# The order of four VectorE products in a frequency-domain convolution, with an MLP behind it

## The chip, the cores and the metric

The kernel runs on one core of a Trainium2 chip. A core has TensorE (matrix products, written to PSUM), VectorE, ScalarE, GpSimd, and SyncE, whose queue issues all DMAs here. Each engine works through its instructions in program order and waits on semaphores for the others. The metric is the device time of one execution in microseconds (us), the median of several runs. A profile of one execution of each kernel is available.

## The reference

Four sequences of 12480 tokens with 128 channels are gated, convolved with a filter made by a small network, gated again, and put through an MLP. The convolution is done by FFT over the sequence:

```python
h_filt = (np.maximum(pos_emb @ w1, 0.0) @ w2) * window      # (S, D), S = 12480, D = 128
u = x * v                                                   # (B, S, D), B = 4
Uf = np.fft.rfft(u, n=2 * S, axis=1)
Hf = np.fft.rfft(h_filt, n=2 * S, axis=0)
y = np.fft.irfft(Uf * Hf[None, :, :], n=2 * S, axis=1)[:, :S, :]
a = x * y                                                   # out of the convolution
h = a @ w_in                                                # 128 -> 2048
out = (h * np.clip(h + 3.0, 0.0, 6.0) / 6.0) @ w_out        # 2048 -> 128
```

## The kernel before

The FFT of length 12544 = 64 x 196 is done as two stages of matrix products with twiddle tables, there and back. Of the 196 frequencies of the long factor, 99 are kept (`K2`), four to a chunk (`CH`), so there are 25 chunks; the last has three. The channels and the batch make 8 groups of 128 columns (2 halves of the sequence x 2 batches x 32 channels). Each group is one *period* (`period`, line 601) of 25 chunks, so that the code around the change runs 200 times.

One chunk (`chunk`, line 629) does this:

- `spectra` (L488) calls `second_stage`: TensorE multiplies four frequencies of the group with the table `tab` (L301) into one PSUM bank, the tile `t`. Its pool is called `s2` and has two buffers, so that chunk n writes the bank of chunk n-2. A bank row holds four frequencies of 128 columns; partitions 0 to 63 hold one part of each complex number and 64 to 127 the other.
- `products` (L503) multiplies with the filter's spectrum `h`. ScalarE first copies the two partition halves crosswise into another PSUM bank, `sw` (L499, and L500 with the sign turned; its pool has one buffer). VectorE then forms four products: `q` and `a` from the spectrum itself (`uv`), `q2` and `a2` from the swapped spectrum (`sv`). `q` and `q2` have 256 columns, `a` and `a2` 512. They read one operand from PSUM and `h` from SBUF. GpSimd adds `q` into half of `a`, `q2` into half of `a2`, and `a2` into `a` (L527). In the first period VectorE does the last of these adds in two chunks of three (L533), a chunk later.
- `third_stage` (L541), three or four chunks later, is the way back: TensorE multiplies `a` with the same table (L546), and ScalarE writes the result over the group's place in `z` (L550).

The order is written out by hand; the instructions are scheduled as they stand. In one chunk: `products` of chunk n, a `third_stage`, `spectra` of chunk n+1, a further `third_stage`. Between the chunks `period` spreads the work of the neighbouring groups: `back` (L552) transposes the finished group before (TensorE L557, ScalarE's copy L560); `visit` (L457) does the first stage of the next group (TensorE L282, ScalarE's copy L294); `fourth_stage` and `results` (L575, L594, L596) finish the group before; `gate_next` (L446) forms x * v on GpSimd (L453) and issues the next loads; `weight` (L647) splits the MLP's weights on VectorE (lines 225 to 247) and ScalarE (L243). `load_h` (L475) issues the two DMAs for the filter's spectrum three chunks ahead, behind the four products; `load_tab` (L465) loads the tables.

Ahead of the periods, `filter` computes the filter's spectrum (to about 158 us); behind them come `last_turn` and the MLP (`Moe.run`, L843), which takes the rest of the time.

The buffers that matter here: `s2` two banks, `sw` one, `s3` two, `ts` three (L267); `a` four tiles in SBUF, `a2`, `q` and `q2` three each; `h` four.

Of the kernel before, what the change touches and what calls it, by code (L numbers as in the profile page):

```python
# [38 lines left out]
GB = 2  # L39
# [211 lines left out]
class Conv:  # L251
# [251 lines left out]
    def products(self, item):  # L503

        nc, P = self.nc, 128
        g, c, kw, t, tab = item
        sw = self.swapped(t, kw)
        hs = self.hs.pop(0)
        a = self.pr.tile([P, CH, 2 * GB, G], F32, tag="a", name="pa", bufs=4)
        a2 = self.pr.tile([P, CH, 2 * GB, G], F32, tag="a2", name="pa2")  # L510
        q = self.pr.tile([P, CH, GB, G], F32, tag="q", name="pq")
        q2 = self.pr.tile([P, CH, GB, G], F32, tag="q2", name="pq2")
        uv = t.rearrange("p (k s g) -> p k s g", k=CH, g=G)[:, :kw]
        sv = sw.rearrange("p (k s g) -> p k s g", k=CH, g=G)[:, :kw]

        def h(ci, si, m):
            return hs[:, ci, :kw, si, :].unsqueeze(2).to_broadcast([P, kw, m, G])

        mul, add = ALU.mult, ALU.add
        nc.vector.tensor_tensor(out=q[:, :kw], in0=uv[:, :, :GB], in1=h(0, 1, GB), op=mul)  # L520
        nc.vector.tensor_tensor(out=a[:, :kw], in0=uv, in1=h(0, 0, 2 * GB), op=mul)  # L521
        nc.vector.tensor_tensor(out=q2[:, :kw], in0=sv[:, :, :GB], in1=h(1, 1, GB), op=mul)
        nc.vector.tensor_tensor(out=a2[:, :kw], in0=sv, in1=h(1, 0, 2 * GB), op=mul)
        self.load_h()

        def plus(x, y):
            nc.gpsimd.tensor_tensor(out=x, in0=x, in1=y, op=add)  # L527

        plus(a[:, :kw, GB:], q[:, :kw])
        plus(a2[:, :kw, GB:], q2[:, :kw])  # L530
        if self.sum:
            s, s2 = self.sum
            nc.vector.tensor_tensor(out=s, in0=s, in1=s2, op=add)  # L533
        self.sum = None
        if g == 0 and c % 3:
            self.sum = a[:, :kw], a2[:, :kw]
        else:
            plus(a[:, :kw], a2[:, :kw])
        return g, c, kw, tab, a
# [355 lines left out]
```

## Time and profile before

| | |
|---|---|
| median of 3 runs | 3170.02 us (3169.38 to 3170.16) |
| profiled execution | 3166.51 us, of which span 3164.7 us |
| TensorE busy | 3114.2 us (98%) |
| ScalarE busy | 2351.7 us (74%) |
| VectorE busy | 2305.8 us (73%) |
| GpSimd busy | 2079.2 us (66%) |
| mean granted TensorE clock | 0.998 |

The span runs from the first instruction of the program to the end of the last. Lines of the profile name an instruction by its line in the kernel's file (L301). A row of a group gives its engine (PE is TensorE, PEld its weight load, DVE is VectorE, ACT is ScalarE, POOL is GpSimd, SP is SyncE), the operation, the tiles written and read, the shape and the count; then the busy time in us, the mean of one in ns, and behind the second bar the time for which the engine stood idle just before, with what ended it. In the order of time a row starts with its start and its length in us, and square brackets hold the idle time ahead of it. What ended a wait is worked out from semaphores: of several, the one that came last is named, and that may be wrong. In names, `pa` is the tile `a` or `a2`, `pq` is `q` or `q2`, `s` a bank of `s2` or `s3`, and `sw` the swapped one.

### The profile page before, as it was taken

What the parts mean: (1) busy time and instruction counts of PE and PEld (TensorE: products, weight loads), DVE (VectorE), ACT (ScalarE), POOL (GpSimd) and SP (SyncE); (2) the same over time, 40 slices, a digit from 0 to 9 for tenths busy, and PEclk for the clock granted to TensorE, in tenths of its full rate; (3) what the DMA queues carried; (4) which work ended last, traced back from release to release, by engine and by line L of the source; (5) the groups of instructions that cost most, each with busy time, mean ns of one, the idle gap of its engine ahead of it and who ended that gap; (6) DMA issues with size and microseconds to landing.
All of it is one profiled execution on the core that took longest, in us unless ns stands there. A gap on an engine that the chain in (4) does not pass through costs nothing.

```text
span 3164.7 us, 53332 instructions
## 1 busy us (share of the span) xinstructions
PE 3114.2 (98%) x19916; PEld 2633.9 (83%) x19916; DVE 2305.8 (73%) x2707; ACT 2351.7 (74%) x3039; POOL 2079.2 (66%) x1240
## 2 busy tenths in 40 slices
PE   9989999999999999999999999999999999999999
PEld 8978888888887788888888888888888888888887
DVE  4467666767654777777777777777777777777776
ACT  2367767767766777878787777777777877777777
POOL 1188777777874666666666666666666666666666
PEclk9999999999999999999999999999999999999999
DMA  6688888787855111111111110111111111111110
GB/s 236 211 205 230 228 230 234 218 238 221 228 172 202 54 36 35 38 42 35 35 40 31 41 41 30 41 39 32 41 36 35 39 32 41 38 33 40 40 31 24
DMA packets 232273, 304.66 MB, mean 96 GB/s; under 512 B 38055, under 2 KB 159310, under 8 KB 231118
## 3 DMA queue, kind: packets, MB, share of 16 engines
q1 hardware_dynamic: 232014, 301.26, 32.6%
q8 instruction: 157, 2.57, 0.3%
q14 instruction: 102, 0.84, 0.1%
HBM read 224.87 MB, written 76.28 MB: 95 GB/s over the span
## 4 chain that ended last, share of the span: by engine, by line
PE 68%; POOL 0%; DVE 0%; ACT 0%; DMA 0%; issue 0%; ACTq 0%
PE acc L827 11%; PE acc L823 11%; PE acc L824 11%; PE ph L788 11%; PE ph L790 11%; PE ph L789 11%; PE ts L575 0%; PE s L557 0%; PE ts L557 0%; POOL pa L527 0%; DMA yd<-y 0%; POOL glo L812 0%; DVE y L596 0%; ACT o L594 0%; ACT ghi L810 0%
## 5 line engine op out<-in xcount | busy, mean ns | idle before, releaser
L812 POOL TENSOR_TENSOR glo<-g,ghi 128x1024 fp32r<-128x1024 f32 x588 | 1404.4, 2397 | 761.2 <-ACT ghi L810 761.0
L800 DVE SCALAR_TENSOR_TENSOR g<-r,ph 128x1024 f32<-128x1024 f32 (+1 forms) x784 | 949.7, 1211 | 408.7 <-ACT r L798 408.3
L798 ACT ACTIVATE r<-ph,three 128x1024 f32<-128x1024 f32 (+1 forms) x784 | 871.1, 1111 | 273.6 <-PE ph L790 273.4
L810 ACT CAST ghi<-g 128x1024 fp32r<-128x1024 f32 (+1 forms) x784 | 811.1, 1035 | 1.9 <-DVE g L800 1.0
L788 PE MATMUL ph<-xhi,win_hi 128*128 128x512 f32 (+1 forms) x1568 | 608.5, 388 | 0.0
L789 PE MATMUL ph<-xlo,win_hi 128*128 128x512 f32 (+1 forms) x1568 | 608.4, 388 | 0.0
L790 PE MATMUL ph<-xhi,win_lo 128*128 128x512 f32 (+1 forms) x1568 | 608.3, 388 | 0.0
L824 PE MATMUL acc<-ghi,wout_lo 128*128 128x512 f32 (+1 forms) x1568 | 608.0, 388 | 0.0
L823 PE MATMUL acc<-ghi,wout_hi 128*128 128x512 f32 (+1 forms) x1568 | 607.9, 388 | 0.0
L827 PE MATMUL acc<-glo,wout_hi 128*128 128x512 f32 (+1 forms) x1568 | 481.3, 388 | 0.6 <-POOL glo L812 0.6
L527 POOL TENSOR_TENSOR pa<-pa,pq 128x256 f32<-128x256 f32 (+1 forms) x400 | 295.6, 747 | 171.3 <-DVE pa L521 133.2
L788 PEld LDWEIGHTS ph<-xhi,win_hi 128*128 128x128 f32 x1568 | 294.4, 188 | 61.5 <-issue 0.8
L827 PEld LDWEIGHTS acc<-glo,wout_hi 128*128 128x128 f32 x1568 | 293.6, 188 | 61.7 <-POOL glo L812 1.5
L824 PEld LDWEIGHTS acc<-ghi,wout_lo 128*128 128x128 f32 x1568 | 294.5, 188 | 60.5
L790 PEld LDWEIGHTS ph<-xhi,win_lo 128*128 128x128 f32 x1568 | 294.4, 188 | 60.5
L823 PEld LDWEIGHTS acc<-ghi,wout_hi 128*128 128x128 f32 x1568 | 294.4, 188 | 60.4
L789 PEld LDWEIGHTS ph<-xlo,win_hi 128*128 128x128 f32 x1568 | 294.5, 188 | 60.4
L812 DVE TENSOR_TENSOR glo<-g,ghi 128x1024 fp32r<-128x1024 f32 x196 | 283.7, 1448 | 0.0
L520 DVE TENSOR_TENSOR pq<-s,h 128x256 f32<-128x256 f32 (+1 forms) x200 | 84.1, 421 | 255.7 <-POOL pa L527 162.2
L761 DVE TENSOR_TENSOR xy<-xt,yt 128x512 f32<-128x512 f32 x96 | 258.7, 2695 | 0.0
L301 PE MATMUL s<-z,tab 128*128 128x128 f32 x1584 | 213.9, 278 | 35.5 <-DVE pa L521 27.9
L527 POOL TENSOR_TENSOR pa<-pa,pa 128x512 f32<-128x512 f32 (+1 forms) x184 | 232.5, 1263 | 14.4
(61 smaller groups left out, 3620.6 us busy)
## 6 DMA issues: line engine op xcount, KB each, us to landing
tab<-in_g_tab SPq DMA_DIRECT2D x192, 256.0 KB
h<-hd SPq DMA_DIRECT2D x384, 128.0 KB
yd<-y SPq DMA_DIRECT2D x64, 512.0 KB
xt<-in_xt SPq DMA_DIRECT2D x98, 256.0 KB
out<-o SPq DMA_DIRECT2D x97, 256.0 KB
xt<-in_x SPq DMA_DIRECT2D x64, 384.0 KB
vt<-in_v SPq DMA_DIRECT2D x64, 384.0 KB
yt<-yd SPq DMA_DIRECT2D x256, 64.0 KB
```

The lines of the kernel that those rows point to most:

```text
L527: nc.gpsimd.tensor_tensor(out=x, in0=x, in1=y, op=add)
L761: self.nc.vector.tensor_tensor(out=xy.rearrange("p (n e c) -> p n e c", e=4, c=GH), in0=xt.rearrange("p (n e c) -> p n e c", e=4, c=GH), i ...
L788: nc.tensor.matmul(ph[:, i, :ne], self.win_hi[:, sl], hi[:, :ne], start=True, stop=False)
L789: nc.tensor.matmul(ph[:, i, :ne], self.win_hi[:, sl], lo[:, :ne], start=False, stop=False)
L790: nc.tensor.matmul(ph[:, i, :ne], self.win_lo[:, sl], hi[:, :ne], start=False, stop=True)
L798: nc.scalar.activation(r[:, :, :ne], ph[:, :, :ne], AF.Relu, bias=self.three)
L800: nc.vector.scalar_tensor_tensor(out=g[:, :, :ne], in0=r[:, :, :ne], scalar=6.0, in1=ph[:, :, :ne], op0=ALU.min, op1=ALU.mult)
L810: nc.scalar.copy(ghi[:, :, :ne], g[:, :, :ne])
L812: e.tensor_tensor(out=glo[:, :, :ne], in0=g[:, :, :ne], in1=ghi[:, :, :ne].bitcast(F32), op=ALU.subtract)
L823: nc.tensor.matmul(a, self.wout_hi[:, f, :], ghi[:, i, :ne], start=(f == 0), stop=False)
L824: nc.tensor.matmul(a, self.wout_lo[:, f, :], ghi[:, i, :ne], start=False, stop=False)
L827: nc.tensor.matmul(a, self.wout_hi[:, f, :], glo[:, i, :ne], start=False, stop=(f == NFC - 1))
```

## The change

The two products of the swapped spectrum are issued first, those of the spectrum itself second, and GpSimd's two first adds change places likewise. Nothing else differs; the operands, the shapes and the buffers are the same.

```diff
@@ -517,17 +517,17 @@
         mul, add = ALU.mult, ALU.add
+        nc.vector.tensor_tensor(out=q2[:, :kw], in0=sv[:, :, :GB], in1=h(1, 1, GB), op=mul)
+        nc.vector.tensor_tensor(out=a2[:, :kw], in0=sv, in1=h(1, 0, 2 * GB), op=mul)
         nc.vector.tensor_tensor(out=q[:, :kw], in0=uv[:, :, :GB], in1=h(0, 1, GB), op=mul)
         nc.vector.tensor_tensor(out=a[:, :kw], in0=uv, in1=h(0, 0, 2 * GB), op=mul)
-        nc.vector.tensor_tensor(out=q2[:, :kw], in0=sv[:, :, :GB], in1=h(1, 1, GB), op=mul)
-        nc.vector.tensor_tensor(out=a2[:, :kw], in0=sv, in1=h(1, 0, 2 * GB), op=mul)
         self.load_h()
 
         def plus(x, y):
             nc.gpsimd.tensor_tensor(out=x, in0=x, in1=y, op=add)
 
+        plus(a2[:, :kw, GB:], q2[:, :kw])
         plus(a[:, :kw, GB:], q[:, :kw])
-        plus(a2[:, :kw, GB:], q2[:, :kw])
         if self.sum:
```

## The prediction, made before the changed kernel had run

> **What bounds the kernel now.** I read the page first, then the busy time by stretches, then the groups by line, then the order of time around single chunks.
>
> ```profile
> span 3164.7 us, 53332 instructions
> 190.00:995.00 805.00, 773.42 (x7825) 679.41 (x7825) 554.02 (x1062) 571.68 (x1086) 629.56 (x617) 0.99 0.79 223
> 463.00:574.00 111.00, 107.75 (x1103) 94.42 (x1102) 78.90 (x149) 79.10 (x151) 86.34 (x84) 0.98 0.82 229
> 1045.00:3100.00 2055.00, 2054.99 (x9110) 1703.68 (x9111) 1594.25 (x1330) 1634.74 (x1710) 1362.74 (x571) 1.00 0.12 37
> ```
>
> The three lower rows give, for a stretch, its length and the busy time of TensorE, its weight loads, VectorE, ScalarE and GpSimd, then the granted clock. In the MLP (1045 to 3100) TensorE never rests, and the edit doesn't touch that code. The edited function runs 200 times (8 periods of 25 chunks), nearly all of it between 190 and 995 us. There TensorE is busy 773.4 of 805.0 us, 96%; GpSimd, the next, 78%. So TensorE paces this stage too, with 31.6 us of rest. A microsecond matters there only if TensorE waits for it.
>
> ```profile
> L301 PE MATMUL s<-z,tab 128*128 128x128 f32 x1584 | 213.9, 278 | 35.5 <-DVE pa L521 27.9 <-issue 3.5 <-ACT raw L243 2.3
> L499 ACT COPY sw<-s 64x512 f32<-64x512 f32 x192 | 107.1, 558 | 107.8 <-DVE pa L523 96.6 <-PE s L301 5.9 <-DVE dec L231 2.8
> L520 DVE TENSOR_TENSOR pq<-s,h 128x256 f32<-128x256 f32 x192 | 81.2, 423 | 236.6 <-POOL pa L527 143.9 <-issue 62.3 <-ACT sw L500 27.9
> L521 DVE TENSOR_TENSOR pa<-s,h 128x512 f32<-128x512 f32 x192 | 130.8, 681 | 0.0
> L522 DVE TENSOR_TENSOR pq<-sw,h 128x256 f32<-128x256 f32 x192 | 79.7, 415 | 0.0
> L523 DVE TENSOR_TENSOR pa<-sw,h 128x512 f32<-128x512 f32 x192 | 130.8, 681 | 0.0
> ```
>
> Two rings are visible. The spectrum's PSUM bank (s2, two buffers) is written by L301, read by ScalarE's two swapping copies and by L520 and L521; L301 of chunk n needs the bank of chunk n-2, and 27.9 of TensorE's 35.5 us of rest at L301 are waits for L521, its last reader. The swapped copy's bank (sw, one buffer) is written by L499 and L500 and read by L522 and L523; ScalarE waits 96.6 us for L523. TensorE's rest hangs on the first ring; the second holds up an engine that has time to spare.
>
> **The change part by part.** It adds and removes no instruction: four products, three adds and two DMA issues per chunk stay. What moves is when the two banks come free. One chunk in order of time, ScalarE, VectorE and TensorE:
>
> ```profile
> 538.23 1.27 ACT L560 COPY w<-ts 99x512 f32<-99x512 f32 x2 [0.98 <-PE ts L557]
> 539.52 0.56 ACT L499 COPY sw<-s 64x512 f32<-64x512 f32 x1
> 540.11 0.57 ACT L500 ACTIVATE sw<-s 64x512 f32<-64x512 f32 x1
> 540.77 0.42 DVE L520 TENSOR_TENSOR pq<-s,h 128x256 f32<-128x256 f32 x1 [2.01 <-POOL pa L527]
> 541.11 0.68 DVE L521 TENSOR_TENSOR pa<-s,h 128x512 f32<-128x512 f32 x1
> 541.71 0.42 DVE L522 TENSOR_TENSOR pq<-sw,h 128x256 f32<-128x256 f32 x1
> 542.04 0.68 DVE L523 TENSOR_TENSOR pa<-sw,h 128x512 f32<-128x512 f32 x1
> 542.07 1.06 PE L301 MATMUL s<-z,tab 128*128 128x128 f32 x8
> ```
>
> *The first product's wait: 0.* One would think that L520, which reads only the bank s2, can run beside the swap, and that the new first product, which needs the swap, begins later. It doesn't: L520 starts at 540.77, 0.09 after L500 ends (540.68), though its operand was ready long before. In 162 of the 200 chunks it starts within 0.11 us of L500's end, in none before it; the first and the last:
>
> ```profile
> 160.40 0.57 ACT L500 ACTIVATE sw<-s 64x512 f32<-64x512 f32 x1
> 161.01 0.42 DVE L520 TENSOR_TENSOR pq<-s,h 128x256 f32<-128x256 f32 x1 [2.50 <-ACT sw L500]
> 990.11 0.46 ACT L500 ACTIVATE sw<-s 64x384 f32<-64x384 f32 x1
> 990.66 0.36 DVE L520 TENSOR_TENSOR pq<-s,h 128x192 f32<-128x192 f32 x1 [1.12 <-POOL pa L527]
> ```
>
> So the wait for both copies stands at the head of the four already, and the release "POOL" named in the row is not the true one. Were it otherwise, both copies (1.13 us) would be added; no chunk shows that.
>
> *The swap's bank comes free earlier.* Its last reader moves from fourth to second: from 542.72 to about 541.79, 0.93 us. ScalarE can use this only where L499 waited for L523.
>
> *The spectrum's bank comes free later.* Its last reader moves from second to fourth, from 541.79 to 542.72: also 0.93 us, here against TensorE. L301 at 542.07 belongs to the chunk two further on and would have to wait until 542.72 + 0.10 = 542.82 (0.10 is the distance that waiting L301s have, below): 0.75 us of rest. Can the earlier swap make up for it? Not in this chunk: L499 at 539.52 starts 0.03 after two copies L560, which waited for TensorE's transposes and not for L523. The same holds for most of the late ones.
>
> All places of one period (chunks 0 to 24, 462.88 to 573.81) where L301 starts less than 1.03 us after its L521 and is not yet pushed out by the place before it (542.07 stands above):
>
> ```profile
> 475.22 0.68 DVE L521 TENSOR_TENSOR pa<-s,h 128x512 f32<-128x512 f32 x1
> 476.16 1.13 PE L301 MATMUL s<-z,tab 128*128 128x128 f32 x8 [0.71 <-DVE pa L521]
> 488.14 0.68 DVE L521 TENSOR_TENSOR pa<-s,h 128x512 f32<-128x512 f32 x1
> 489.10 1.11 PE L301 MATMUL s<-z,tab 128*128 128x128 f32 x8
> 501.72 0.68 DVE L521 TENSOR_TENSOR pa<-s,h 128x512 f32<-128x512 f32 x1
> 502.71 1.06 PE L301 MATMUL s<-z,tab 128*128 128x128 f32 x8
> 513.96 0.68 DVE L521 TENSOR_TENSOR pa<-s,h 128x512 f32<-128x512 f32 x1
> 515.60 1.06 PE L301 MATMUL s<-z,tab 128*128 128x128 f32 x8
> 528.33 0.68 DVE L521 TENSOR_TENSOR pa<-s,h 128x512 f32<-128x512 f32 x1
> 529.11 1.13 PE L301 MATMUL s<-z,tab 128*128 128x128 f32 x8 [0.47 <-ACT raw L243]
> 551.52 0.68 DVE L521 TENSOR_TENSOR pa<-s,h 128x512 f32<-128x512 f32 x1
> 552.48 1.06 PE L301 MATMUL s<-z,tab 128*128 128x128 f32 x8
> 566.71 0.68 DVE L521 TENSOR_TENSOR pa<-s,h 128x512 f32<-128x512 f32 x1
> 567.49 0.91 PE L301 MATMUL s<-z,tab 128*128 128x128 f32 x6
> ```
>
> L301's distance from the end of its L521 is 0.26, 0.28, 0.31, 0.96, 0.10, 0.28, 0.28 and 0.10 (in order of time, 542.07 sixth). The waiting ones show 0.10 (529.11) and 0.26 (476.16) as the least. A place that waits already moves by the whole 0.93; another by 1.03 less its distance, or 1.19 less it, capped at 0.93, where the longer least applies. I take 0.93, 0.91 (0.28 counted as the longer kind), 0.72, 0.07, 0.93, 0.75, 0.75, 0.93: 6.0 us a period, between 5.7 and 6.4 by the choice of least.
>
> Do they add up? L301 of chunk n is pushed only relative to the products of n-2. These hang, through L560, on transposes that TensorE does after L301 of n-2, so they carry all delays up to n-2, but none of n-1. Late places two or more chunks apart therefore add; neighbours don't, which is why 557.16, one chunk after 552.48, isn't in the list. Carried so through all 200 chunks, crediting each swap with what it gains, the periods give 7.4, 6.4, 6.2, 6.0, 6.0, 6.0, 5.7, 5.3: 49 us from 66 places, these the first and last:
>
> ```profile
> 162.28 1.13 PE L301 MATMUL s<-z,tab 128*128 128x128 f32 x8 [1.66 <-DVE pa L521]
> 985.57 0.91 PE L301 MATMUL s<-z,tab 128*128 128x128 f32 x6
> 989.62 0.45 ACT L499 COPY sw<-s 64x384 f32<-64x384 f32 x1 [0.66 <-DVE pa L523]
> ```
>
> The third row is the last swap: it waits 0.66 us for L523 and leads to the last adds and the end of the stage, so here the earlier release pays. With the swaps before it I credit 2 us. Sum: 49 - 2 = +47 us.
>
> *The rest: 0.* GpSimd's first add still follows the second product, its second the fourth; loads of h still follow the fourth product, so SyncE's queue passes nothing new. The reuse of the product buffers (three or four chunks back) has microseconds to spare. Cover for all this is TensorE; where TensorE itself waits longer, they only gain time.
>
> *A rule.* The Trainium skill, Perfetto Trace Analysis, section Optimization Strategy, says that a gap which repeats on the engine that should be saturated can mean too little SBUF or PSUM for the next tile. The repeating gap at L301 agrees (27.9 us). Read for the swap's single bank instead, it speaks for the change; that is the first rival.
>
> The profiled execution took 3166.51 us, 1.8 more than its span, and becomes 3213.5; the median of the runs lies 3.5 above it, so 3170.0 + 47 = **3217 us**.
>
> **The rivals.**
>
> *The single bank decides: faster, 3138.* Where ScalarE waits for L523 in chunk after chunk, the swap's ring takes two copies, four products and the hand-overs, 1.13 + 0.09 + 1.95 + 0.09 = 3.26 us a chunk; the change cuts it to 2.33, and the advances could add up from chunk to chunk. Once L499 ahead of a late L301 starts more than 0.93 us earlier, the bank s2 comes free sooner than now in spite of its later place, and at the most the stage's 31.6 us of TensorE's rest go: 3138. For it: the 96.6 us. Against it: at 539.52 the swap follows L560 by 0.03, and TensorE, not the ring, sets L560. By the skill's rule just named, read for this bank, the time would be this one. Chance 0.06.
>
> *The two cancel: no change, 3170.* If each such L499 starts 0.93 us earlier and no more, the fourth product ends when the second did, and no L301 moves. The same row speaks against it; some places (989.62) have it. Chance 0.07.
>
> *Half: 3197.* If the products hang on TensorE's work four chunks back rather than two, late places in a row hide behind each other; counted so, 27 remain. Chance 0.14.
>
> *More: 3235.* If nothing is credited to earlier swaps and neighbours add too, 83 places give 65. Chance 0.07.
>
> **How the numbers follow.** Forecast 0.66, spread 3205 to 3226. I reach down to 3192 to take in most of the half case and up to 3230 for a part of the more case: about 0.8 in all. A measurement of this kernel tells 0.2%, 6 us, from no change. Faster 0.06; same 0.07; slower 0.87.
>
> **What would show it.** In the changed kernel lines 520 and 521 are the swapped products, 522 and 523 those of the spectrum itself. Right if: TensorE's rest at L301 grows from 35 to about 80 us, released by L523; ScalarE's wait at L499 falls by more than half; the first product still starts 0.09 after L500; the MLP's stretch is as long as before and starts some 47 us later. Wrong if L301's rest stays under 45 us (cancelled), lies near 60 (half), or if L499 starts earlier ahead of the late L301s (first rival), or if the first product comes over 0.2 us after L500 where VectorE was free.

## The result and the profile after

| | before | changed |
|---|---|---|
| median | 3169.70 us | 3204.35 us |
| all runs | 3169.18 to 3170.16 | 3202.23 to 3205.09 |
| profiled execution | 3166.51 us, span 3164.7 | 3205.09 us, span 3203.3 |

The ratio is 1.0107, with a 95% interval of 1.0091 to 1.0123: the changed kernel is 34.65 us slower. Between the two profiled spans lie 38.6 us; the profile of before was taken in an execution 3.2 us below its median.

The page's first line, the busy time by stretches (length, busy TensorE, weight loads, VectorE, ScalarE, GpSimd, granted clock) and the groups by line, all of the changed kernel; behind them two groups of the kernel before for comparison:

```profile
span 3203.3 us, 53401 instructions
190.00:1033.00 843.00, 779.35 (x7834) 681.41 (x7833) 559.72 (x1065) 585.73 (x1086) 629.57 (x618) 1.00 0.75 214
L301 PE MATMUL s<-z,tab 128*128 128x128 f32 x1584 | 218.4, 281 | 69.1 <-ACT sw L499 31.5 <-DVE pa L523 21.9 <-DMA yd<-y 8.2
L499 ACT COPY sw<-s 64x512 f32<-64x512 f32 (+1 forms) x200 | 110.8, 554 | 37.6 <-DVE pa L521 22.6 <-PE s L546 4.6 <-PE s L301 4.5
L546 PE MATMUL s<-pa,tab 128*128 128x128 f32 x1584 | 216.6, 280 | 1.3 <-DVE pa L533 0.9 <-POOL pa L527 0.3
```

```profile
L499 ACT COPY sw<-s 64x512 f32<-64x512 f32 (+1 forms) x200 | 110.8, 554 | 108.7 <-DVE pa L523 97.3 <-PE s L301 5.9 <-DVE dec L231 2.8
L546 PE MATMUL s<-pa,tab 128*128 128x128 f32 x1584 | 216.6, 280 | 2.3 <-POOL pa L527 1.4 <-DVE pa L533 1.0
```

The stage that ended near 995 us now ends near 1033. TensorE's busy time in it grew by 5.9 us, its rest from 31.6 to 63.7 us. L301's own rows grew by 4.5 us (213.9 to 218.4): eight of them that follow a rest are shown as 1.13 us, eight that follow other work as 1.06. The rest stands where it stood before, at L301 (35.5 to 69.1 us), and not at L546 (2.3 to 1.3 us), the next matmul that waits for VectorE's and GpSimd's work. ScalarE's wait at L499 fell from 108.7 us to 37.6 us. What is behind the convolution has the same length: the last write of `z`, at 994.98 before and at 1033.55 after, is followed by 2169.7 us in both.

The chunk that the prediction worked out (L301 at 542.07 before), in the order of time of the changed kernel. Lines 520 and 521 are now the products of the swapped spectrum, 522 and 523 those of the spectrum itself:

```profile
555.57 1.27 ACT L560 COPY w<-ts 99x512 f32<-99x512 f32 x2 [0.98 <-PE ts L557]
556.86 0.56 ACT L499 COPY sw<-s 64x512 f32<-64x512 f32 x1
557.45 0.57 ACT L500 ACTIVATE sw<-s 64x512 f32<-64x512 f32 x1
558.11 0.42 DVE L520 TENSOR_TENSOR pq<-sw,h 128x256 f32<-128x256 f32 x1 [2.01 <-POOL pa L527]
558.45 0.68 DVE L521 TENSOR_TENSOR pa<-sw,h 128x512 f32<-128x512 f32 x1
559.05 0.41 DVE L522 TENSOR_TENSOR pq<-s,h 128x256 f32<-128x256 f32 x1
559.33 0.56 ACT L499 COPY sw<-s 64x512 f32<-64x512 f32 x1
559.38 0.68 DVE L523 TENSOR_TENSOR pa<-s,h 128x512 f32<-128x512 f32 x1
560.16 1.13 PE L301 MATMUL s<-z,tab 128*128 128x128 f32 x8 [0.59 <-ACT sw L499]
```

The first swap follows L560 by 0.02 us, as before, and the first product follows L500 by 0.09. The next swap (559.33) begins while the products still run: that is the swapped bank coming free early. But L301 begins 0.10 us after L523 ends (560.06), with 0.59 us of rest ahead of it. The releaser in its brackets, L499, is a misreading: that copy had ended at 559.89, and L523 was the later. Read by its start against the ends around it, the row names its true cause; by the brackets alone one would blame ScalarE.

### The profile page after: what moved, and what is told of

Same layout as the page of the kernel before. It is cut to its first block, busy times and chain, and to the rows that moved or that the text cites. A ratio compares the mean times of both kernels' runs of the same rounds, so it can differ in the third digit from the quotient of the medians.

```text
span 3203.3 us, 53401 instructions
## 1 busy us (share of the span) xinstructions
PE 3120.2 (97%) x19916; PEld 2634.7 (82%) x19916; DVE 2311.1 (72%) x2707; ACT 2366.1 (74%) x3039; POOL 2080.5 (65%) x1240
## 4 chain that ended last, share of the span: by engine, by line
PE 72%; ACT 1%; DVE 0%; issue 0%; DMA 0%; POOL 0%; SPq 0%; DVEq 0%; POOLq 0%; ACTq 0%
PE acc L827 11%; PE acc L823 11%; PE acc L824 11%; PE ph L788 11%; PE ph L790 11%; PE ph L789 11%; PE ts L557 2%; PE ts L575 1%; PE s L301 1%; PE s L546 1%; PE ts L282 1%; PE s L557 0%; ACT w L560 0%; ACT sw L499 0%; DMA yd<-y 0%
## 5 line engine op out<-in xcount | busy, mean ns | idle before, releaser
L520 DVE TENSOR_TENSOR pq<-sw,h 128x256 f32<-128x256 f32 (+1 forms) x200 | 83.8, 419 | 283.8 <-POOL pa L527 147.7
L301 PE MATMUL s<-z,tab 128*128 128x128 f32 x1584 | 218.4, 281 | 69.1 <-ACT sw L499 31.5
L301 PEld LDWEIGHTS s<-z,tab 128*128 128x128 f32 x1584 | 195.3, 194 | 81.6 <-ACT sw L499 76.9
```

Of the source, the lines that this page charges most:

```text
L301: self.nc.tensor.matmul(t[:, i * 128 : (i + 1) * 128], tab[:, i, :], z[:, c * CH + i, :], start=True, stop=True)
```

## The experiments

Theory **H**: the rise comes from the spectrum's bank s2 being held 0.93 us longer, through L301. Rivals: **S**, the time follows the swap's single bank; **A**, the swapped order costs in itself; **G**, the order of GpSimd's adds costs. All ratios are against the kernel before, run beside them.

| kernel | median us | ratio, 95% interval |
|---|---|---|
| GpSimd's adds exchanged only | 3197.43 | 1.0083, 1.0067 to 1.0100 |
| VectorE's products exchanged only | 3231.05 | 1.0190, 1.0175 to 1.0205 |
| order q2, q, a, a2 | 3196.39 | 1.0081, 1.0066 to 1.0096 |
| spectrum's products ahead of the copies | 3288.91 | 1.0376, 1.0361 to 1.0391 |
| s2 three banks, old order | 3180.83 | 1.0033, 1.0021 to 1.0044 |
| s2 three banks, new order | 3162.03 | 0.9973, 0.9962 to 0.9984 |
| sw two banks, old order | 3174.94 | 1.0015, 1.0006 to 1.0024 |
| sw two banks, new order | 3205.39 | 1.0110, 1.0093 to 1.0127 |
| no weight splitting, old order | 3199.08 | 1.0094, 1.0079 to 1.0109 |
| same, adds exchanged only | 3203.70 | 1.0113, 1.0098 to 1.0128 |
| same, order q2, q, a, a2 | 3214.62 | 1.0142, 1.0125 to 1.0159 |
| same, the change | 3235.87 | 1.0206, 1.0191 to 1.0221 |

### The two halves of the change apart

Only the adds, against the kernel before:

```diff
-        plus(a[:, :kw, GB:], q[:, :kw])
         plus(a2[:, :kw, GB:], q2[:, :kw])
+        plus(a[:, :kw, GB:], q[:, :kw])
```

> VectorE's products in the order of before; only GpSimd's two first adds change places. Theory H (how long the spectrum's bank s2 is held decides: L301 waits for its last reader): s2's last reader does not move, so 3170 within 4 us. Rival G (the order of the adds decides: the first add now waits for the fourth product, and TensorE's L546 behind it): the whole rise of the change, about 3204, with TensorE's rest at L546 instead of L301.

Only the products, with the adds as before:

```diff
+        nc.vector.tensor_tensor(out=q2[:, :kw], in0=sv[:, :, :GB], in1=h(1, 1, GB), op=mul)
+        nc.vector.tensor_tensor(out=a2[:, :kw], in0=sv, in1=h(1, 0, 2 * GB), op=mul)
         nc.vector.tensor_tensor(out=q[:, :kw], in0=uv[:, :, :GB], in1=h(0, 1, GB), op=mul)
         nc.vector.tensor_tensor(out=a[:, :kw], in0=uv, in1=h(0, 0, 2 * GB), op=mul)
-        nc.vector.tensor_tensor(out=q2[:, :kw], in0=sv[:, :, :GB], in1=h(1, 1, GB), op=mul)
-        nc.vector.tensor_tensor(out=a2[:, :kw], in0=sv, in1=h(1, 0, 2 * GB), op=mul)
```

> VectorE's products in the order of the change; GpSimd's adds in the order of before, so the first add waits for the fourth product and the second is free already. H: as the change, 3204 within 5 us, rest at L301 about 69 us. G: near 3170.

Measured, beside a median of 3170.98 for the kernel before: +26 and +60 us. Both expectations failed. Yet the four kernels form a table whose rows agree. With the adds in the order of the products, exchanging both costs 34.65 us. With the adds the other way round, the products cost 3231.05 - 3197.43 = 33.6 us. So the products carry the change's rise, and a mismatch of adds and products costs another 26 us, in either order. Neither H nor G had that. The groups by line show where the adds' part arises, first before, then with the adds alone exchanged:

```profile
L225 DVE TENSOR_SCALAR dec<-raw 128x256 int32<-128x256 int32 x16 | 14.8, 926 | 0.0
L237 DVE TENSOR_SCALAR dec<-raw 128x256 int32<-128x256 int32 x16 | 9.6, 597 | 0.0
```

```profile
L225 DVE TENSOR_SCALAR dec<-raw 128x256 int32<-128x256 int32 x16 | 27.1, 1692 | 0.0
L237 DVE TENSOR_SCALAR dec<-raw 128x256 int32<-128x256 int32 x16 | 18.7, 1170 | 0.0
L301 PE MATMUL s<-z,tab 128*128 128x128 f32 x1584 | 215.5, 279 | 57.8 <-DVE pa L521 25.4 <-issue 18.8 <-ACT raw L243 8.5
L546 PE MATMUL s<-pa,tab 128*128 128x128 f32 x1584 | 217.4, 280 | 3.0 <-POOL pa L527 1.7 <-DVE pa L533 1.0
```

Of VectorE's steps of the weight splitting (`dec`), which touch SBUF alone, these two take nearly twice as long. Not all do (L235 fell from 1127 to 704 ns); all eleven together rose from 122.0 to 147.8 us. TensorE rests more at L301 (35.5 to 57.8 us), not at L546. Where the first add waits for the fourth product, the adds run just when VectorE turns to the splitting. One such place in the same kernel, in order of time:

```profile
504.39 2.36 POOL L453 TENSOR_TENSOR u<-xt,vt 98x1024 f32<-98x1024 f32 x1
506.71 1.42 POOL L527 TENSOR_TENSOR pa<-pa,pq 128x256 f32<-128x256 f32 x2
508.21 1.28 POOL L527 TENSOR_TENSOR pa<-pa,pa 128x512 f32<-128x512 f32 x1
505.98 2.30 DVE L225 TENSOR_SCALAR dec<-raw 128x256 int32<-128x256 int32 x1
508.32 1.32 DVE L227 TENSOR_SCALAR dec<-dec 128x256 f32<-128x256 f32 x1
509.56 0.28 DVE L229 TENSOR_SCALAR dec<-raw 128x256 int32<-128x256 int32 x1
```

GpSimd is at work almost without a break from 504.39 to 509.49. L225 and L227 take 2.30 and 1.32 us beside it, each ending 0.15 us after one of its rows, and L229, a step of the same shape, takes 0.28 once GpSimd is done. The next chunk's products stand behind these steps, and L301 behind the products. The Trainium skill, SBUF — State Buffer, section Who interferes with whom, has this: VectorE and GpSimd share a pair of SBUF ports, copies and tensor_scalar in their two-port modes take it whole, and whichever comes second is blocked until the other ends. These rows agree with it in the order of the ends; that the port is the cause was not tried by itself. (Theory **C**: the 26 us come from the splitting's steps beside GpSimd. What of it passes through TensorE's clock is in the last section.)

### A smaller delay of the bank

```diff
-        nc.vector.tensor_tensor(out=q[:, :kw], in0=uv[:, :, :GB], in1=h(0, 1, GB), op=mul)
-        nc.vector.tensor_tensor(out=a[:, :kw], in0=uv, in1=h(0, 0, 2 * GB), op=mul)
         nc.vector.tensor_tensor(out=q2[:, :kw], in0=sv[:, :, :GB], in1=h(1, 1, GB), op=mul)
+        nc.vector.tensor_tensor(out=q[:, :kw], in0=uv[:, :, :GB], in1=h(0, 1, GB), op=mul)
+        nc.vector.tensor_tensor(out=a[:, :kw], in0=uv, in1=h(0, 0, 2 * GB), op=mul)
         nc.vector.tensor_tensor(out=a2[:, :kw], in0=sv, in1=h(1, 0, 2 * GB), op=mul)
```

> Order q2, q, a, a2: the spectrum's last reader moves from second to third (one 0.33 us product later), the swapped bank's last reader stays fourth. H: the same walk through the rows of before as in the prediction, with 0.33 in place of 0.93 and no credit for the swap, gives 16 us: 3186, between 3180 and 3190. Rival S (the time follows when the swap's bank comes free, or the swapped product's coming first): S by the bank gives 3170, S by the first place gives all of the change, 3204.

Measured: +25 us, above the range. S is out by the bank (it gave none) and unlikely by the first place (it gave 34). The splitting's L225 takes 1579 ns here against 926, so part of the 25 may be C again; the first add now waits for the third product. The runs without splitting, below, separate the two.

### The spectrum's products ahead of the copies

```diff
-        sw = self.swapped(t, kw)
         hs = self.hs.pop(0)
...
-        sv = sw.rearrange("p (k s g) -> p k s g", k=CH, g=G)[:, :kw]
...
         nc.vector.tensor_tensor(out=q[:, :kw], in0=uv[:, :, :GB], in1=h(0, 1, GB), op=mul)
         nc.vector.tensor_tensor(out=a[:, :kw], in0=uv, in1=h(0, 0, 2 * GB), op=mul)
+        sw = self.swapped(t, kw)
+        sv = sw.rearrange("p (k s g) -> p k s g", k=CH, g=G)[:, :kw]
```

> The spectrum's two products are issued ahead of ScalarE's two copies, which then wait for them; the swapped products follow. The spectrum's last reader is then L500, some 1.1 us before the second product of before ends, if the copies start when they did. H: the walk through the rows, with TensorE's rest at L301 shrinking where it is pushed less, gives up to -25 us: 3145, between 3140 and 3165; rest at L301 falls from 35 to about 10 us. If rest once there is never given back, as the prediction's sum had it: 3170. S: the swap's bank comes free where it did, 3170; if ScalarE's copies get late behind the products, slower than 3170.

Measured: +118 us. H's forecast of 3140 to 3165 failed; what was named last in the expectation came, and large. The groups by line of that kernel (the product `a` stands in line 519 there):

```profile
L499 ACT COPY sw<-s 64x512 f32<-64x512 f32 (+1 forms) x200 | 110.8, 554 | 249.0 <-DVE pa L519 246.9 <-ACT w L560 0.3
L282 PE MATMUL ts<-ctab,u 98*64 98x99 f32 (+1 forms) x5120 | 260.6, 261 | 61.5 <-ACT w L560 50.1 <-ACT z L294 10.8 <-DVE u L365 0.5
```

ScalarE now waits 247 us for VectorE's product (before, 97 us for L523), which itself stands behind the earlier chunk's work in VectorE's queue; the copies L560 and L294 queued behind L499 hold up TensorE at L282 (0.6 us before). So here the bank that ScalarE and VectorE read in turn couples their queues, and the order decides which of them waits. This run doesn't test H: ScalarE's copies, now the bank's last readers, were late themselves (rest at L301 is 44.1 us, 41.3 of it put down to L500).

### Three banks for the spectrum, two for the swap

The four pools hold eight banks together (2 + 1 + 2 + 3). The sum is kept: the third stage's pool `s3` gives one up. Each pool size was run in both orders, the one of before and the one of the change:

```diff
-    BANKS = {"s2": 2, "sw": 1, "s3": 2, "ts": 3}
+    BANKS = {"s2": 3, "sw": 1, "s3": 1, "ts": 3}
```

> The order of before, with three banks for the spectrum (s2) and one for the way back (s3). This is the partner of the next run. H: TensorE's rest at L301 released by VectorE goes, but the single s3 bank can bring waits at L546 for L550: between 3145 and 3220.

> The order of the change (products and adds), with the same banks, s2 three and s3 one. H: L301 needs the bank of three chunks back, about 4 us more to spare than the 0.93 us by which its last reader moved, so the difference to its partner is gone: within 5 us of it, or up to 12 us faster by the swap's bank that comes free earlier. Rival A (the swapped order costs in itself: its first wait, VectorE's or GpSimd's time): 34 us slower than its partner, as with two banks.

```diff
-    BANKS = {"s2": 2, "sw": 1, "s3": 2, "ts": 3}
+    BANKS = {"s2": 2, "sw": 2, "s3": 1, "ts": 3}
```

> The order of before, with two banks for the swap (sw) and one for the way back (s3). Partner of the next run. ScalarE's wait of 97 us at L499 for L523 goes. H: little of it reaches TensorE; against the run with three s2 banks and the same order (same s3) it is slower or equal, by up to 20 us.

> The order of the change with sw two and s3 one. H: the spectrum's bank is still held 0.93 us longer and the swap's bank matters to neither, so the difference to its partner is at least that of the change and up to the walk's sum without credit for the swap: 34 to 52 us slower than its partner. Rival S (the time follows the swap's single bank): no difference.

With three s2 banks the change no longer costs anything: it is 18.8 us *faster* than its partner (3162.03 against 3180.83), more than the 12 us at most that were expected. With two sw banks it costs 30.5 us (3205.39 against 3174.94), a little below the 34 to 52 expected. One more expectation failed: with the old order, two sw banks were to be no faster than three s2 banks, and were 5.9 us faster (3174.94 against 3180.83). A is out, since the same order gains in one case; S is out, since a second sw bank leaves the rise nearly whole. In the groups by line, three s2 banks with the old order and then with the new:

```profile
L301 PE MATMUL s<-z,tab 128*128 128x128 f32 x1584 | 210.3, 276 | 1.5 <-DVE pa L521 0.8 <-issue 0.7
L546 PE MATMUL s<-pa,tab 128*128 128x128 f32 x1584 | 221.6, 283 | 25.4 <-ACT z L550 22.5 <-POOL pa L527 1.7
L282 PE MATMUL ts<-ctab,u 98*64 98x99 f32 (+1 forms) x5120 | 236.9, 249 | 16.6 <-ACT w L560 13.8 <-ACT z L294 2.3 <-DVE u L365 0.5
```

```profile
L301 PE MATMUL s<-z,tab 128*128 128x128 f32 x1584 | 210.4, 276 | 6.7 <-DMA tab<-in_g_tab 4.3 <-DVE pa L523 1.7 <-issue 0.7
L546 PE MATMUL s<-pa,tab 128*128 128x128 f32 x1584 | 220.8, 282 | 22.2 <-ACT z L550 18.2 <-POOL pa L527 2.3 <-DVE pa L533 1.5
L282 PE MATMUL ts<-ctab,u 98*64 98x99 f32 (+1 forms) x5120 | 234.1, 249 | 2.5 <-ACT w L560 2.0 <-DVE u L365 0.5
```

L301 hardly waits in either (4.3 of the 6.7 us are for a load). With the old order the swap's ring then reaches TensorE another way: ScalarE, waiting at L499 for the single sw bank (108.8 us), is late with its copies L560, and L282 waits 16.6 us; the new order cuts the two waits to 43.4 and 2.5. With two sw banks and the old order L282 waits 0.5 us, which fits the 5.9 us: the swap's bank does matter to TensorE there. So the earlier release is worth something, once the later release costs nothing. The new order with three s2 banks beats both kernels by a little: 0.9973 of before.

### Without the weight splitting

In all four kernels the load of the MLP's weights and the twelve steps are left out, and zeros stored in their place:

```diff
-    n = NW
...
-    nc.vector.tensor_tensor(out=lo.bitcast(F32R), in0=a, in1=s, op=ALU.add)
-    yield
+    for i in range(12):
+        yield
...
-            load_words(self.nc, raw, src)
-            buf = self.dp.tile([128, 3 * NW], F32, tag="dec", name="dec")
-            self.steps = decode(self.nc, raw, buf[:, : 2 * NW], buf[:, 2 * NW :])
+            self.nc.vector.memset(raw, 0.0)
+            self.steps = decode(self.nc, raw, None, None)
```

> The kernel before without the splitting of the MLP's weights inside the periods: the weights' load and the twelve steps on VectorE and ScalarE are left out, and a tile of zeros is stored in their place, so the output is zero. Partner of the next three runs; 3140 to 3170.

> As its partner, with only GpSimd's two first adds exchanged. Theory C (the 26 us that this exchange cost came from VectorE's weight splitting, whose steps took longer when GpSimd's adds ran beside them): nothing left, within 5 us of the partner. Rival G (the adds' later end holds up TensorE at L546): 20 to 30 us slower.

> As the partner, with the products in the order q2, q, a, a2. H with C: the part of its 25 us that the walk gave, 16 us, stays and the rest goes: 11 to 19 us slower than the partner. If all of the 25 us came from the bank held longer: 22 to 28 us slower.

> As the partner, with the change (products and adds). H: the rise stays, 28 to 40 us slower than the partner, about twice that of the order q2, q, a, a2. If the weight splitting carries the change's rise too: under 10 us.

The partner itself was slower than expected, 3199.08 us. One likely part: VectorE's memset of the tile waits for the store of the tile before it, as the waits of that kernel show (us in total, times, longest); it holds VectorE's queue, in all four kernels alike (69 to 79 us at the memset in all).

```profile
DVE raw L623 <- DMA wd<-raw: 52.2, 5, 10.7
```

TensorE's clock is another part: it is halved for 44.4 us of the partner's convolution, against 13.7 in the full kernel, which costs at most half of the difference, 15.4 us. In the other three it is halved for 41.0 (adds), 37.5 and 37.5 us, so the clock doesn't make them slower than their partner.

Against this partner, the adds alone cost 4.6 us (26 with the splitting; the two intervals against the kernel before overlap, so 4.6 isn't clear of the scatter), the smaller delay 15.5 us (25 with it; 16 forecast), and the change 36.8 us. Theory C holds for the adds: most of their cost went with the splitting. H holds for the rest: a hold longer by 0.33 us costs 15.5 us, and one longer by 0.93 us costs 36.8 us. The partner is 29 us slower than the full kernel, so the sizes carry over only roughly.

## Why the prediction was right, and where its size was off

Right were the sign and the mechanism: +47 us were forecast, +34.65 measured, 38.6 between the profiles. The size owes something to luck. 3204.35 lies just below the spread of 3205 to 3226, in the part of the range that was added for the half case, and it is nearer to that rival's 3197 than to 3217. TensorE's rest at L301, 69.1 us, lies midway between the two cases' signs (60 and 80). The time alone doesn't tell them apart; the places one by one do.

- *The first product's wait, 0.* It follows L500 within 0.11 us in 155 of 200 chunks, against 162 before.
- *The late places.* In the period whose rows the prediction showed, the first two L301s move by 0.93 and 0.91 us (forecast 0.93 and 0.91), the third by 0.42 (0.72), then by 0.07 (0.07), 0.98 (0.93), 0.75 and 0.75 (0.75 and 0.75). Late places two or three chunks apart add up here, against the half case. Only the last place fails, 0.24 us for 0.93 (below).
- *Rest at L301.* About 80 us expected, 69.1 found.
- *The tail.* Two us were credited; the last L301 moves by 39.65 us, the end of the stage by 38.57: 1.1 us.
- *GpSimd and the reuse of buffers, 0.* L546's rest didn't grow. But the cost of nothing for GpSimd was right only because the change keeps adds and products in step; the prediction didn't see that the adds' place beside VectorE's splitting mattered (26 us).

The step that failed in size is "Do they add up?". It let each push of L301 stay for good, with only pushes by neighbours hiding each other. Two things were overlooked: TensorE's own rest, where there was some, shrinks when its work comes later (the first period), and a chunk's products can hang on VectorE's queue instead of on TensorE (the last place of the middle periods). Period by period (shift between each period's first L301 and the next one's, and the stage's end for the last; 1.1 us of shift stood there before the first chunk):

| period | 0 | 1 | 2 | 3 | 4 | 5 | 6 | 7 |
|---|---|---|---|---|---|---|---|---|
| forecast, us | 7.4 | 6.4 | 6.2 | 6.0 | 6.0 | 6.0 | 5.7 | 5.3, less 2 |
| measured, us | 2.0 | 5.1 | 5.7 | 5.1 | 5.1 | 5.1 | 5.8 | 3.7 |

The first period makes 5.4 us of the 9.4 by which these sums differ, periods 1 to 5 another 4.5; the last two came out 0.5 larger than forecast. In the first period, two neighbouring L301s and the swap on which the second hangs, in order of time, before and then after:

```profile
186.14 1.13 PE L301 MATMUL s<-z,tab 128*128 128x128 f32 x8
187.08 0.56 ACT L499 COPY sw<-s 64x512 f32<-64x512 f32 x1 [1.59 <-DVE pa L523]
189.55 1.13 PE L301 MATMUL s<-z,tab 128*128 128x128 f32 x8 [1.39 <-DVE pa L521]
```

```profile
188.41 0.56 ACT L499 COPY sw<-s 64x512 f32<-64x512 f32 x1 [0.66 <-PE s L546]
189.33 1.13 PE L301 MATMUL s<-z,tab 128*128 128x128 f32 x8 [0.92 <-ACT sw L499]
191.81 1.13 PE L301 MATMUL s<-z,tab 128*128 128x128 f32 x8 [0.46 <-DVE pa L523]
```

The first L301 is pushed by 3.19 us in all, 0.93 of it here. The second stood 1.39 us idle before; it now stands 0.46, so the 0.93 is given back at once, and its shift is 2.26. It could come that early because its swap, which had waited 1.59 us for the single sw bank, waits 0.66. So it goes from chunk to chunk in that period. This is the mechanism of the rival "The two cancel", at work in one period of eight.

In periods 3 to 5 the shortfall is the last place, chunk 24, and no rest shrinks there. In period 4, the end of the splitting, the products of chunk 22 behind it and the L301 of chunk 24, before and then after:

```profile
676.98 0.43 DVE L247 TENSOR_TENSOR raw<-dec 128x256 fp32r<-128x256 f32 x1
677.32 0.42 DVE L520 TENSOR_TENSOR pq<-s,h 128x256 f32<-128x256 f32 x1
678.43 0.91 PE L301 MATMUL s<-z,tab 128*128 128x128 f32 x6 [1.41 <-issue]
```

```profile
700.28 0.42 DVE L247 TENSOR_TENSOR raw<-dec 128x256 fp32r<-128x256 f32 x1
700.62 0.42 DVE L520 TENSOR_TENSOR pq<-sw,h 128x256 f32<-128x256 f32 x1
702.66 0.91 PE L301 MATMUL s<-z,tab 128*128 128x128 f32 x6 [1.41 <-ACT sw L499]
```

The products start right behind L247 in both kernels, so their shift, 23.30 us, is that of VectorE's queue. With 0.93 more it gives 24.23, which is L301's shift. But L301 of chunk 21 had shifted by 23.98 already: the push hides behind the ones before it, as in the half case, and adds 0.25. The prediction had the products hang on TensorE's transposes, through L560, and so carry every delay up to chunk 22. (In periods 3 and 5 the clock of the kernel before is halved just there, so the rows look different; the products of chunk 22 shift as little, 4.4 us within the period.)

Against the medians 4 us more are left: the profile of before was taken below its median, that of the changed kernel 0.7 us above.

## What to carry to other kernels

When two products read two banks, ask for each bank who waits for its *last* reader and whether that engine sets the pace: here, taking most of a wait of 97 us off ScalarE cost TensorE 34 us. Delays of a pacing engine are summed with its present rests taken off, place by place, and for each place one asks which queue its releaser hangs on. With a spare bank for the engine that paces, the same edit turned from a loss into a gain here.

## What the runs showed of the hardware

TensorE's granted clock halves for stretches of 3.41 us or a small multiple of it (up to 10.24 us). In the kernel before one begins at 558.2, after the rest of 2.06 us that ends at 557.16; the busy times of three neighbouring stretches, with the granted clock third from the end:

```profile
554.00:558.00 4.00, 1.94 (x17) 1.78 (x17) 3.97 (x9) 1.36 (x3) 2.08 (x3) 1.00 0.73 244
558.00:562.00 4.00, 4.00 (x46) 3.73 (x46) 3.93 (x7) 2.65 (x6) 3.92 (x3) 0.57 0.42 120
562.00:566.00 4.00, 4.00 (x52) 3.87 (x49) 3.96 (x5) 3.17 (x7) 3.30 (x4) 1.00 0.62 183
```

In the kernels before and after, and in the one with the adds exchanged, TensorE was busy for 0.30 to 0.51 of the 3.41 us ahead of each halving in the convolution (from the trace's record of the granted clock and its matmuls). Of the other windows of 3.41 us, counted on in the same step from halving to halving, none has under 0.52. The Trainium skill, TensorE: Matmul & The Clock Gate, Part 1, says that the gate returns to half rate after a window of some 3.4 us of idleness; here rest in half a window or a little more was enough, so the trace is stricter than the rule.

The halvings of the convolution add up to 13.7 us before and also 13.7 us after, so they are no part of the change's rise. In the kernel with the adds exchanged they are 30.7 us: half of the 17.1 us more, 8.5 us, is the most that they can add to its 26 us. With the products alone exchanged they are 41.0 us (at most 13.7 of the 60 us), with the spectrum's products ahead of the copies 102.4 us (at most 44 of the 118). A rest of some two microseconds can thus cost more than its own length.
